# Four small moves in the first third of an attention-and-FFN kernel: one copy changes engine, three groups of loads change place

## The chip, the cores and the metric

The kernel runs on one core of a Trainium2 chip. A core has five instruction streams that run side by side and meet only through semaphores: TensorE (PE in the profile; its weight loads are listed apart as PEld), VectorE (DVE), ScalarE (ACT), GpSimd (POOL) and SyncE (SP). Each stream runs its instructions strictly in the order in which the program issues them, so an instruction that waits holds up everything behind it on its own engine and nothing on the others. Data comes in and goes out by DMA. This program issues DMAs from two places: from SP (queue q1 of the profile, "hardware_dynamic") and from POOL (queue q0, "software_dynamic"); both are served by the same 16 DMA engines. The metric is the device time of one execution in microseconds (us); lower is better.

## The reference

Two blocks follow each other. The first is attention with a selective decay, for batch 8, 8 heads, 576 positions, head dimension 64:

```python
scores = scale * np.matmul(q, k.transpose(0, 1, 3, 2))
causal = np.triu(np.ones((S, S), dtype=bool), k=1)
cum = np.cumsum(np.maximum(s, 0.0), axis=-1)
bias = -(cum[:, :, :, None] - cum[:, :, None, :])
scores = np.where(causal, -1000000000.0, scores + np.minimum(bias, 0.0))
attn = softmax(scores)
attn_out = np.matmul(attn, v)
```

Its output, 4608 rows of 512, goes into a gated FFN with inner width 1536:

```python
g = x @ w_gate
val = x @ w_val
out = (silu(g) * val) @ w_out
```

## The kernel before

**Attention.** The 64 (batch, head) pairs are numbered 0 to 63, and four of them make a group; there are 16 groups, and `h` in `side` and `side_v` is the number of the group whose scores are being made, `step` (0 to 3) the pair in it, `ci` (0 to 3) the piece of that pair's scores. "k 3" or "q 3" is the k or q of group 3, "V 1" the values of batch 1. A group's k and q are loaded as f32 (`load_one`, L141), cast to bf16 (`cast_one`, L253), transposed, and copied into a tile `KQ` in SBUF that holds rows ready for the scores. For groups 0 to 4 TensorE transposes (`pe_transpose`, L295, its matmuls at L301) and `pe_out` (L319) copies the result out of PSUM, at L330 on VectorE or at L328 on ScalarE, in two halves of 64 partitions; a bank of PSUM is given back after its second half. From group 5 on the transposes are done by DMA: `scratch` (L272, L274) writes the cast tile to DRAM, `transposes` (L281, L284) reads it back transposed, and `split` (L286, L288) copies it into `KQ`. The scores are matmuls at L373, their exponentials are on ScalarE at L383 (into a tile `pt`), and GpSimd clears the masked triangles at L388 and L393.

V is loaded in five pieces a batch (`load_v`, L156): four of 128 positions (256 KB) and one of 64 (128 KB), all in rows of 256 bytes. There is one raw buffer for V, so V of the next batch can be loaded only when the last piece of the one before is cast. `cast_v` (L167) casts the pieces: V 1 and V 2 on GpSimd (L173), V 3 and later on ScalarE (L171). The weighted sums are matmuls at L410, in five parts a pair: parts 0 to 2, part 3, part 4, the last of which need V pieces 3 and 4. The result reaches the FFN's input `XT` by TensorE for batches 0 and 1 (`x_pe`, L453, L459), and later by a write to DRAM (L444) and a DMA transpose (L451).

**FFN.** The 4608 rows are taken in nine tiles of 512. For each tile 12 column blocks follow (`gate_value`, L658): four matmuls for the gate (L643), a tanh on ScalarE (`th`, L664), a multiply on VectorE (`pp`, L666), four matmuls for the value (L643), a multiply on VectorE (`ht`, L677). Then comes the down product (L700 for the first two tiles, L749 later). The weights are loaded by `w_load` (L335, issued at L346): the gate's first half in one piece (768 KB), then the value's first half in two, then the second halves of gate and value in two pieces each ("1, 0" and "1, 1", 384 KB each), then `w_out` in two of 768 KB. Column blocks 6 to 8 use the pieces "1, 0", blocks 9 to 11 the pieces "1, 1".

**Order.** The order of the instructions is written out by hand. Eight banks of PSUM are handed round (`take`, `give`): a new product gets the bank that was given back longest ago, and TensorE waits until its reader is done. A prologue (L949 to L1036) makes the first eight pairs of attention and begins the first FFN tile. After it the FFN's tiles are driven as a list of items (L1060 to L1090); after each item the loop runs at most one delayed copy (`seconds`), the hooks of that item, and then pumps the attention generator `attn_items` (L561), so that attention for later rows is woven between the FFN's matmuls. The hooks of the first tile are the transposes of k 2's second part at item 2, the casts of k 3 and q 3 on GpSimd at items 9 and 10, and the two loads of `w_out` on GpSimd's queue at items 11 and 13.

`prep_one` (L540) makes one set of a group's TensorE transposes and its first copy, and puts the second copy on the list `seconds`:

```python
pe_out(hb, nm, g, 0, eng)
seconds.append(lambda: pe_out(hb, nm, g, 1, eng))
```

Around the change, in order: V 1 is loaded from SP at L1015, followed by k, q 4 and k, q 5; V 1 is cast on GpSimd beside the scores of pairs 11 and 12 (`V1_AT`, L477); pair 8's weighted sums, the first that need V 1, follow the scores of pair 12. Later, at `h == 6`, SP issues the loads of k 9 and q 9 at step 0, the write of group 8 at step 2, the first two pieces of V 4 at step 2, the transposes of group 8 and the last three pieces of V 4 at step 3; ScalarE casts k 9 and q 9 at `h == 7`, steps 0 and 1.

Of the kernel before, what the change touches and what calls it, by code (L numbers as in the profile page):

```python
# [19 lines left out]
def kernel(  # L20
# [11 lines left out]
    nc = tc.nc  # L32
# [81 lines left out]
    with tc.manual_schedule():  # L114
# [16 lines left out]
        def give(b):  # L131
            clock[0] += 1
            released[b] = clock[0]
# [7 lines left out]
        def load_one(hb, name, rs=(0, NR), eng=nc.sync):  # L141
            b, g = divmod(hb, 2)
            if rs[0] == 0:
                loaded[name, hb] = raw.tile([128, NR, J, D], FP32, tag="raw" + name, name="raw" + name)
            eng.dma_start(
                loaded[name, hb][:, rs[0] : rs[1], :, :].rearrange("x r j d -> x r (j d)"),
                SRC[name][0][b, g * HB + 2 * rs[0] : g * HB + 2 * rs[1], :, :].rearrange(
                    "(r e) (p j) d -> (e p) r (j d)", e=2, j=J
                ),
            )  # L150

        def load_qk(hb):
            load_one(hb, "k")
            load_one(hb, "q")

        def load_v(b, cs, eng=nc.sync):  # L156
            if 0 in cs:
                loaded["v", b] = raw.tile([128, NCH, H, D], FP32, tag="rawv", bufs=1, name="rawv")
            t = loaded["v", b]
            for c in cs:  # L160
                n = 128 if c < 4 else TAIL
                eng.dma_start(  # L162
                    t[0:n, c, :, :],
                    v[b, :, c * 128 : c * 128 + n, :].rearrange("h p d -> p h d"),
                )
# [153 lines left out]
        def pe_out(hb, name, g, r, eng):  # L319
            j0, j1 = JG[g]  # L320
            kq = SRC[name][1]
            dst = KQ[hb % 2][r][64 * r : 64 * r + 64, kq, 0 : NR * S].rearrange(
                "a (x j) -> a x j", j=J
            )[:, :, j0:j1]
            tp = tps[name, g]
            srcp = tp[0][64 * r : 64 * r + 64].rearrange("a j x -> a x j")
            if eng is nc.scalar:
                nc.scalar.copy(dst, srcp)  # L328
            else:
                eng.tensor_copy(dst, srcp)  # L330
            tp[2] -= 1
            if tp[2] == 0:
                give(tp[1])

        def w_load(kind, j, h=None):  # L335
            dst = {"g": WG, "v": WV, "o": WO}[kind][j]
            if kind == "o":
                src_ap = moe_w_out[j * WKO * 128 : (j + 1) * WKO * 128, :].rearrange(
                    "(c p) n -> p c n", p=128
                )  # L340
            else:
                w = moe_w_gate if kind == "g" else moe_w_val
                lo, hi = (0, WCH) if h is None else (h * WCH // 2, (h + 1) * WCH // 2)
                src_ap = w[:, j * WCH + lo : j * WCH + hi].rearrange("(c p) n -> p c n", p=128)
                dst = dst[:, :, lo:hi]
            nc.gpsimd.dma_start(dst, src_ap)  # L346
# [124 lines left out]
        def do_later(n):  # L471
            while n > 0 and later:
                f, *args = later.pop(0)
                f(*args)
                n -= 1
# [5 lines left out]
        def side(h, step, ci):  # L481
            bh = HB * h + step
            for c in V1_AT.get((bh, ci), ()):
                cast_v(1, c, nc.gpsimd)
            if bh == H + 4 and ci == 3:
                load_v(2, range(5))
            if h == 4 and (step, ci) in ((0, 1), (2, 1)):
                load_qk(6 + step // 2)
            if h >= 5 and h + 3 < NHB and (step, ci) == (0, 1):
                load_qk(h + 3)  # L490
            hb = h + 1
            if NPE <= hb < NHB:
                late = hb == NPE
                if late and (step, ci) == (0, 1):
                    scratch(hb)
                if late and (step, ci) == (0, 3):
                    transposes(hb)
                if (step, ci) == (0, 1):
                    aug(hb, GP4)
                first = 1 if hb < NPE + 3 else 0  # L500
                if step in (first, first + 1) and ci == (3 if late else 1):
                    for r in range(NR):
                        later.append((split, hb, "kq"[step - first], r))
            hb = h + 2
            if hb == NPE and step == 3 and ci % 2 == 1:
                cast_one(hb, "kq"[ci // 2], nc.gpsimd)
            if NPE < hb < NHB:
                six = hb == NPE + 1
                if (step, ci) == ((2, 0) if six else (0, 2)):
                    cast_one(hb, "k", nc.scalar)  # L510
                if (step, ci) == ((2, 2) if six else (1, 2)):
                    cast_one(hb, "q", nc.scalar)
                if (step, ci) == ((3, 0) if six else (2, 0)):
                    scratch(hb)
                if (step, ci) == (3, 3 if six else 0):
                    do_later(NR * 2)
                    transposes(hb)
            if ci != 1:
                return
            bn = h // 2 + 1  # L520
            if 3 <= bn < B:
                if h % 2 == 0:
                    if step == 2:
                        load_v(bn, (0, 1))
                    if step == 3:
                        load_v(bn, (2, 3, 4))

        V2_AT = {(1, 0): 0, (1, 1): 1, (1, 2): 2, (1, 3): 3, (2, 0): 4}
# [1 line left out]

        def side_v(h, step, ci):
            bn = h // 2 + 1
            if h == 4 and (step, ci) in V2_AT:
                cast_v(2, V2_AT[step, ci], nc.gpsimd)
            if 3 <= bn < B and h % 2 == 1 and (step, ci) in V_AT:
                cast_v(bn, V_AT[step, ci], nc.scalar)

        seconds = []

        def prep_one(hb, i, eng=None):  # L540
            g, nm = divmod(i, 2)
            nm = ("k", "q")[nm]
            pe_transpose(hb, nm, g)
            if eng is None:
                eng = nc.scalar if nm == "k" else nc.vector
            pe_out(hb, nm, g, 0, eng)
            seconds.append(lambda: pe_out(hb, nm, g, 1, eng))

        PREP_AT = {
            2: {(1, 3): 0, (2, 1): 2, (2, 3): 1, (3, 1): 3},  # L550
# [432 lines left out]
        load_one(2, "q", eng=nc.gpsimd)  # L983
        w_load("v", 0, 0)
        w_load("v", 0, 1)
        for nm in ("g", "v"):
            w_load(nm, 1, 0)
        load_one(3, "k", eng=nc.gpsimd)
        scores(1)
        half_batch("k")  # L990
        score_piece(2, 0)
# [9 lines left out]
        aug(2, SP4)  # L1001
        cast_one(2, "k", nc.gpsimd)
        cast_one(2, "q", nc.gpsimd)
        load_one(3, "q", eng=nc.gpsimd)
        for nm in ("g", "v"):
            w_load(nm, 1, 1)
        init_vt(1)
# [21 lines left out]
            seconds.pop(0)()  # L1029
        for ft in range(3):  # L1030
            begin("g", ft, range(2, 3))
        for i in (1, 3):
            prep_one(2, i)
        first_sbuf.close()
        PTP[0] = ctx.enter_context(tc.tile_pool(name="later", bufs=1))
        PTP["bufs"] = 5  # L1036
# [85 lines left out]
```

## Time and profile before

| what | value |
|---|---|
| times of three runs | 373.49, 375.02, 375.54 us; median 375.02 us |
| the profiled execution's own time | 374.06 us |
| its span, first to last instruction | 372.1 us |
| busy: PE, DVE, ACT, POOL | 361.0, 289.8, 240.9, 212.3 us |
| mean granted TensorE clock | 0.998 |
| DMA packets, and those under 512 B | 97134, 77229 |

The span is what the trace covers; what lies outside it is 1.96 us. Times inside the trace are counted from the start of the span. An entry of the chain of waits or of the timeline has its start, its length, the engine and the line; a bracket at its end tells how long the engine had been idle and what ended that. An entry for a DMA queue has the number of packets, the megabytes and the share of the 16 engines' time. One row of V is a packet of 256 bytes.

### The profile page before, as it was taken

Reading aid. Unit: us, or ns where it says so; the run is one execution under the profiler, and the core shown is the slowest. Engines: PE = TensorE matmul, PEld = TensorE weight load, DVE = VectorE, ACT = ScalarE, POOL = GpSimd, SP = SyncE. Lnnn points to the kernel's source line nnn. Section 1 sums busy time; section 2 is a strip of 40 time slices with the busy share of each in tenths; the row PEclk is TensorE's granted clock in tenths of the full one; section 3 lists DMA queues with packets and bytes.
Section 4 is the critical chain, followed back from the end, with each engine's and each line's share of the span. In section 5 each row is a group of like instructions: output and inputs, shape, how many; then the busy total and the mean of one; then the engine's idle time right before and its main releaser. Section 6 shows DMA issues by size and latency. Waiting matters only on the chain.

```text
span 372.1 us, 8744 instructions
## 1 busy us (share of the span) xinstructions
PE 361.0 (97%) x3248; PEld 230.3 (62%) x3288; DVE 289.8 (78%) x584; ACT 240.9 (65%) x471; POOL 212.3 (57%) x325
## 2 busy tenths in 40 slices
PE   7799999999999999999999999999999999999996
PEld 6574557655555557855685558655865585476465
DVE  8878776377995999589967897699868867975984
ACT  8877776788885977688757875786565523323321
POOL 7984555956266647594749464955675516315320
PEclk9999999999999999999999999999999999999999
DMA  7999999799979996896789575995142113002003
GB/s 241 200 256 258 217 261 267 215 315 225 273 153 322 220 247 185 152 300 211 214 179 263 166 192 166 252 177 138 40 121 62 35 29 119 0 2 87 28 0 113
DMA packets 97134, 64.21 MB, mean 173 GB/s; under 512 B 77229, under 2 KB 82725, under 8 KB 97093
## 3 DMA queue, kind: packets, MB, share of 16 engines
q1 hardware_dynamic: 84964, 41.46, 46.7%
q0 software_dynamic: 12128, 22.21, 23.2%
q8 instruction: 25, 0.41, 0.5%
q14 instruction: 17, 0.13, 0.1%
HBM read 37.90 MB, written 19.86 MB: 155 GB/s over the span
## 4 chain that ended last, share of the span: by engine, by line
PE 86%; DVE 5%; POOL 3%; ACT 2%; issue 1%; DMA 1%; SPq 0%; DVEq 0%; ACTq 0%; POOLq 0%
PE banks L643 45%; PE banks L749 17%; PE banks L373 10%; PE banks L410 8%; PE banks L700 5%; DVE kq L330 2%; DVE pp L666 1%; DMA rawk<-in_k_dram 1%; POOL rawv L162 1%; DVE ht L677 1%; POOL vt L173 1%; PE banks L301 1%; ACT pt L383 1%; PE banks L459 1%; ACT th L664 0%
## 5 line engine op out<-in xcount | busy, mean ns | idle before, releaser
L383 ACT ACTIVATE pt<-banks 128x512 bf16<-128x512 f32 (+1 forms) x256 | 120.5, 509 | 29.2 <-PE banks L373 16.8
L643 PE MATMUL banks<-XT,wg 128*128 128x512 bf16 x418 | 110.3, 379 | 1.2 <-DVE pp L666 0.3
L643 PE MATMUL banks<-XT,wv 128*128 128x512 bf16 x412 | 109.3, 379 | 1.1
L664 ACT ACTIVATE th<-banks 128x512 bf16<-128x512 f32 x108 | 64.7, 599 | 56.2 <-PE banks L643 50.3
L666 DVE SCALAR_TENSOR_TENSOR pp<-th,banks 128x512 bf16<-128x512 bf16 x108 | 73.6, 682 | 18.5 <-ACT th L664 18.0
L677 DVE SCALAR_TENSOR_TENSOR ht<-pp,banks 128x512 bf16<-128x512 bf16 x108 | 74.1, 686 | 10.3
L373 PE MATMUL banks<-kq 128*128 128x128 bf16 (+4 forms) x576 | 76.5, 240 | 0.9 <-DVE kq L330 0.3
L686 POOL TENSOR_TENSOR ht<-ht 128x512 bf16<-128x512 bf16 x35 | 40.4, 1154 | 52.3 <-DVE su L684 52.2
L373 PEld LDWEIGHTS <-kq 128*128 128x128 bf16 x576 | 46.1, 98 | 30.5 <-issue 1.7
L643 PEld LDWEIGHTS <-wv 128*128 128x128 bf16 x432 | 38.4, 98 | 36.2 <-issue 0.2
L643 PEld LDWEIGHTS <-wg 128*128 128x128 bf16 x432 | 38.3, 98 | 34.2 <-issue 0.7
L410 PEld LDWEIGHTS <-pt 128*128 128x128 bf16 x960 | 41.9, 98 | 17.1
L388 POOL TENSOR_SCALAR_AFFINE_SELECT pt<-pt 128x512 bf16<-128x512 bf16 x56 | 36.9, 658 | 25.8 <-ACT pt L383 21.9
L410 PE MATMUL banks<-vt,pt 128*128 128x65 bf16 x960 | 46.9, 194 | 0.1
L444 POOL DMA_DIRECT2D xs<-ot x24 | 21.7, 904 | 30.5 <-DVE ot L427 28.2
L749 PEld LDWEIGHTS <-ht 128*128 128x128 bf16 x336 | 31.2, 98 | 4.3
L427 DVE TENSOR_TENSOR ot<-banks,rc 128x320 bf16<-128x320 f32 x64 | 31.5, 492 | 2.2
L188 POOL DMA_DIRECT2D kq<-HL x48 | 28.9, 605 | 0.0
L749 PEld LDWEIGHTS <-su 128*128 128x128 bf16 x252 | 23.5, 98 | 3.3
L700 PE MATMUL banks<-wo,ht 128*128 128x512 bf16 x90 | 24.8, 379 | 0.3
L814 POOL TENSOR_TENSOR ysb<-ysb 128x512 f32<-128x512 f32 x12 | 15.2, 1270 | 15.3 <-DVE ysb L808 15.3
L749 PE MATMUL banks<-WS,ht 128*128 128x256 bf16 x168 | 22.9, 273 | 0.0
(101 smaller groups left out, 376.7 us busy)
## 6 DMA issues: line engine op xcount, KB each, us to landing
out_dram<-ysb POOLq DMA_DIRECT2D x32, 256.0 KB, 4.0
rawv<-in_v_dram SPq DMA_DIRECT2D x28, 256.0 KB
rawk<-in_k_dram SPq DMA_DIRECT2D x12, 576.0 KB
rawq<-in_q_dram SPq DMA_DIRECT2D x12, 576.0 KB
xs<-ot POOLq DMA_DIRECT2D x24, 160.0 KB, 4.0
ks<-ck SPq DMA_DIRECT2D x11, 288.0 KB
qs<-cq SPq DMA_DIRECT2D x11, 288.0 KB
rawk<-in_k_dram POOLq DMA_DIRECT2D x3, 576.0 KB, 5.6
```

Of the source, the lines that this page charges most:

```text
L373: nc.tensor.matmul(sc[:, o : o + w], T[:, 1, e * S + 128 * tj : e * S + 128 * (tj + 1)], T[:, 0, e * S + lo : e * S + hi], start=not maske ...
L383: nc.scalar.activation(pt[:, c0 : c0 + n], sc, AF.Exp, scale=0.125)
L388: nc.gpsimd.affine_select(pt[:, 1088:1600], pt[:, 1088:1600], pattern=[[0, 4], [1, 128]], compare_op=ALU.is_ge, fill=zreg, base=0, channel ...
L410: nc.tensor.matmul(av[:, bi * (D + 1) : (bi + 1) * (D + 1)], pt[:, c0 : c0 + 128], VT[b % 2][:, tj, h, :], start=(tj == 0), stop=(tj == bi),)
L427: nc.vector.tensor_mul(ot[:, :, e * D : (e + 1) * D], av3[:, :, 0:D], rc[:, :, None].to_broadcast([128, NCH, D]),)
L643: nc.tensor.matmul(view(bs, TT), w[:, c, f0 : f0 + 128], xt[:, c, :], start=(c == 0), stop=(c == 3),)
L664: nc.scalar.activation(th, pg, AF.Tanh, scale=0.5)
L666: nc.vector.scalar_tensor_tensor(pp, in0=th, scalar=1.0, in1=pg, op0=ALU.add, op1=ALU.mult)
L677: nc.vector.scalar_tensor_tensor(hp[:, 2 * k2 : 2 * k2 + 2, :].rearrange("p a n -> p (a n)"), in0=pp, scalar=0.5, in1=pv, op0=ALU.mult, op ...
L686: (nc.vector if ft == NFT - 1 else nc.gpsimd).tensor_sub(hp[:, 1:3, :], hp[:, 1:4:2, :], hp[:, 0:3:2, :])
L700: nc.tensor.matmul(view(pys[ts_], DM), hps[ft // 2][:, 2 * (ft % 2) + half, c0 : c0 + 128], WO[j][:, ft % WKO, :], start=(ft == 0), stop=( ...
L749: nc.tensor.matmul(ps, lhs(p), rhs(p), start=(first and p == 0), stop=(last and p == NP - 1), skip_group_check=True,)
```

## The change

Four things are edited. (1) `prep_one` takes a second engine for the second copy; the last of q 2's copies, of the second 64 partitions of its second part, is made by ScalarE where VectorE made it. (2) The loads of k 3 and q 3 on GpSimd's queue are both issued after the value weights' first half and in front of the third pieces of the gate and the value ("1, 0"); before, k 3 stood behind these two pieces, and q 3 behind the casts of k 2 and q 2. (3) The first two pieces of V 4 are loaded at the last score piece of `h == 5`, in place of `h == 6`, step 2. (4) q 9 is loaded at `h == 6`, step 3, in front of the last three pieces of V 4; before, it was loaded at step 0, right behind k 9, which stays there.

```diff
@@ side
             if h >= 5 and h + 3 < NHB and (step, ci) == (0, 1):
-                load_qk(h + 3)
+                if h == 6:
+                    load_one(h + 3, "k")
+                else:
+                    load_qk(h + 3)
...
             if 3 <= bn < B:
                 if h % 2 == 0:
-                    if step == 2:
+                    if step == 2 and h != 6:
                         load_v(bn, (0, 1))
                     if step == 3:
+                        if h == 6:
+                            load_one(h + 3, "q")
                         load_v(bn, (2, 3, 4))
@@ side_v
             bn = h // 2 + 1
+            if h == 5 and (step, ci) == (3, 3):
+                load_v(4, (0, 1))
@@ prep_one
-        def prep_one(hb, i, eng=None):
+        def prep_one(hb, i, eng=None, eng2=None):
...
-            seconds.append(lambda: pe_out(hb, nm, g, 1, eng))
+            seconds.append(lambda: pe_out(hb, nm, g, 1, eng2 or eng))
@@ the prologue
         w_load("v", 0, 0)
         w_load("v", 0, 1)
+        for nm in ("k", "q"):
+            load_one(3, nm, eng=nc.gpsimd)
         for nm in ("g", "v"):
             w_load(nm, 1, 0)
-        load_one(3, "k", eng=nc.gpsimd)
         scores(1)
...
         cast_one(2, "k", nc.gpsimd)
         cast_one(2, "q", nc.gpsimd)
-        load_one(3, "q", eng=nc.gpsimd)
...
-        for i in (1, 3):
-            prep_one(2, i)
+        prep_one(2, 1)
+        prep_one(2, 3, None, nc.scalar)
```

## The prediction

> **What bounds the kernel now.** I read the page's busy times and chain first, then TensorE's waits, then each place where the change acts.
>
> ```profile
> PE 361.0 (97%) x3248; PEld 230.3 (62%) x3288; DVE 289.8 (78%) x584; ACT 240.9 (65%) x471; POOL 212.3 (57%) x325
> PE 86%; DVE 5%; POOL 3%; ACT 2%; issue 1%; DMA 1%; SPq 0%; DVEq 0%; ACTq 0%; POOLq 0%
> ```
>
> TensorE bounds the whole, so an edit is worth what it takes from, or adds to, TensorE's waits. Between 26 and 300 us the view of waits shows only three for it, 0.3 us each. The timeline places the two that matter:
>
> ```profile
> 33.43 0.38 PE L373 MATMUL banks<-kq 128*128 128x320 bf16 x2 [0.31 <-DVE kq L330]
> 34.15 1.02 PE L643 MATMUL banks<-XT,wg 128*128 128x512 bf16 x3 [0.34 <-DVE pp L666]
> ```
>
> The chain of waits (start, length, what) shows why: from 29 to 35.5 us it runs through VectorE, whose copies and products give back the banks that TensorE waits for. Its later lines show a second weak place at 52 us.
>
> ```profile
> 29.03 1.44 DVE kq L330 x2
> ...
> 32.66 0.72 DVE kq L330
> ...
> 33.41 0.70 DVE pp L666
> ...
> 34.20 0.69 DVE ht L677
> ...
> 34.89 0.61 DVE pp L666
> ...
> 35.54 1.89 PE banks L643 x8
> ...
> 50.89 1.13 POOL vt L173 x2
> ...
> 52.06 0.19 PE banks L410
> ```
>
> The copy at 32.66 is the one that edit 1 moves. The last two lines say that pair 8's weighted sums wait for GpSimd's cast of V 1: V 1 has almost nothing to spare.
>
> GpSimd's timeline shows what edit 2 removes, two casts that wait for their loads, and what stands behind them on that engine: the first load of w_out.
>
> ```profile
> 37.96 1.14 POOL L260 CAST ck<-rawk 128x1152 bf16<-128x1152 f32 x1 [0.79 <-DMA rawk<-in_k_dram]
> ...
> 39.41 1.15 POOL L260 CAST cq<-rawq 128x1152 bf16<-128x1152 f32 x1 [0.30 <-DMA rawq<-in_q_dram]
> ...
> 40.69 0.85 POOL L346 DMA_DIRECT2D wo<-in_moe_w_out_dram  x1
> ```
>
> Last, the DMA view in three stretches. From 34 to 42 us the two queues get the same number of packets, whatever their size:
>
> ```profile
> q0 software_dynamic: 1243, 1.83, 91.7%
> q1 hardware_dynamic: 1252, 0.31, 27.1%
> ```
>
> From 42 to 44.5 us POOL's queue has run nearly dry (the weights are in, w_out's rows not yet there), and V 1, on q1, rushes through:
>
> ```profile
> q1 hardware_dynamic: 1669, 0.42, 79.7%
> q0 software_dynamic: 233, 0.18, 46.2%
> ```
>
> From 46 to 50 us w_out and V 1's last piece alternate again:
>
> ```profile
> q0 software_dynamic: 635, 0.63, 93.6%
> q1 hardware_dynamic: 547, 0.18, 28.5%
> ```
>
> **Edit 1, the copy.** It takes one 64x512 copy off VectorE (0.72 us, the row at 32.66) and puts one on ScalarE (0.72 us, L328's rows of 64x512). Everything VectorE does behind it moves up by that and its 0.03 us of issue: the product at 33.41 to 32.66. On ScalarE the copy falls between the tanh that ends at 30.24 and the k 2 copy at 30.56, so the two tanhs behind (31.15, 32.50) end at about 32.15 and 33.50. The first is early enough for the product at 32.66; the second allows the next product at about 34.15 in place of 34.81. TensorE's block at 35.54, which waited for that product, starts at about 34.87: a gain of 0.67, call it 0.65. ScalarE is back in step at the tanh of 37.52, before which it idles 1.05 us. Bounds: 0 if ScalarE's 0.4 us lateness reaches the banks, 1.0 if both waits and the gap at 35.5 vanish.
>
> **Edit 2, the order of loads.** Two 576 KB loads pass two of 384 KB. GpSimd issues the same instructions; k 2's cast moves 0.75 us back (one issue), to end near 25.4, while the cast of q 2 waits for its load until 26.41 anyway: cost nothing. "1, 0" of the gate and value, issued at 21.31 and 22.04, landed 12.1 and 14.1 us later (33.4, 36.2); behind k 3 and q 3 that is some 3.2 us later (those two landed 1.7 and 1.5 us apart, 37.9 and 39.4 by issue plus 15.1 and 11.9), so 36.6 and 39.4. TensorE needs them at 40.82 and 42.34, or 0.65 sooner: 2.3 us of cover at the tightest; if it were gone, TensorE would stand by the shortfall. k 3 and q 3 are in before 35 us, the casts follow GpSimd's mask work at about 36.5 and 37.6, the mask at L393 must await ScalarE to about 38.85, and the first w_out load is issued at about 39.1 in place of 40.69. The casts' waits themselves cost TensorE nothing; without the edit they would eat about half of edit 1's gain.
>
> But the earlier w_out load speaks against the change. Before, its first rows move about 2.8 us after its issue, near 43.5; now from about 42, when the queue still holds weights. The hole closes, and V 1 keeps taking turns. By 42 us V 1 has had about 2,250 of its 4,608 packets (2,282 of q1 from 28 to 42, a few of them other). In front of it stand some 150 weight packets and w_out's 1,536, at 635 in 4 us: 10.6 us, to 52.6. V 1 gets as many turns less a little, some 1,500 to 1,690, and the rest (670 to 850) at the 667 per us of the hole: the last piece is in at about 53.8, where before it was in at 50 (547 more packets of q1 by then). Its cast, the third of the casts from 50.84, started at about 52.0 and would with edit 1 start at 51.3; now it starts at 53.8 and ends 0.6 later. TensorE's part 4 of pair 8 began at 52.95 and now begins at about 54.45: 1.5 us later than before, with edit 1's gain already in it. Piece 3 says the same: its last packet passes near 52.8, its cast ends at 53.5, and part 3, which began at 52.06, begins 1.5 late. Behind it, k 4 and q 4 come after V 1 on q1: GpSimd already waits for them at 54.44 (1.61 us) and 56.95 (1.36 us), and they too slip, by no more than 1.5 to 2 us. What comes later is bound by TensorE and moves along. Bounds: -0.65 (half of the hole survives; 0.75 us of lateness is enough to close it, and I expect 1.6), and +2.6 if V 1's last engine ends 1 us after the others, as k 4's cast suggests: it starts 1.7 us after k 4's last packets near 52.7.
>
> The Trainium skill ("DMA: Bandwidth & Descriptors", "Latency and other measured facts") puts the first byte of such a software-issued DMA about 1 us after its issue. By that w_out would have been in the queue at 41.7 before, no hole would have been there to lose, and the sum would be edit 1's alone, 373.9; the packets from 42 to 44.5 us show the hole, so the trace speaks against it here.
>
> **Edits 3 and 4.** Near 113 to 127 us TensorE waits for nothing, so no gain. V 4's two issues (1.83 us at 113.18) go in front of XT's transposes at 105.90, and q 9's 0.46 us leaves 109.06; SP is then about 1.3 us late at L451, covered by the 1.6 us between the last such packets (115.5) and the FFN tile that reads them (117.10). q 9 now follows SP's transposes of group 8 (issues from 118.32 to 123.16), so it is issued near 121.5 to 123, behind their packets, and lands near 125 to 127; its cast runs at 126.77 on ScalarE. Cost: 0 to 1 us of ScalarE, which idles 0.6 to 0.8 us at a time there; I take 0, as the nearest rows (k 9 and q 9 both through in 5 us from 108.43) land it just in time. V 4's last three pieces stand behind q 9 but are cast only from 131.37.
>
> **The sum.** The profiled execution took 374.06 (span 372.1 and 1.96 around it). Edit 1: -0.65; V 1 late: +2.15; the rest 0: +1.5, 375.6. The median shown is 0.96 above that execution; the mean of all four executions is 374.5, and with +1.5 I forecast 376.0.
>
> **The rivals.** *The hole doesn't matter* (not slower): w_out starts no earlier than V 1 can bear, and edit 1's gain stays: 374.5 - 0.65 = 373.9. For it: half of the hole is enough; against it: the wait of GpSimd is plainly in front of the load. It decides at a w_out issue about 0.5 us earlier than before; from 0.75 the hole is gone. The skill's rule above belongs here. *ScalarE starves at q 9*: SP's transposes go at 118.32 as before, q 9 lands at 127.5 or later, ScalarE holds scores and tanhs for 1 to 2 us, and TensorE loses up to that: on top of V 1's, 377.5. For it: a load with some 5 us for a way that took 5; against it: ScalarE idles there. *Edit 1 does nothing*, because ScalarE's own tanhs come 0.4 late: 375.2 without V 1's loss, inside the first rival's range.
>
> **How the numbers follow.** V 1 late 0.50, hole harmless 0.38, q 9 late 0.12. A measurement of this kernel tells about 0.5% (1.9 us) from no change, so faster is under 373.1 and slower over 376.9. V 1 late spans 374.4 to 377.8 (its bounds): a third of it, 0.16, is slower, 0.34 within. The harmless case spans 372.8 to 375: 0.16 faster, 0.22 within. q 9 late: 0.09 slower, 0.03 within. Together 0.16, 0.59, 0.25. The range for 8 in 10 is 373.2 to 377.8; the likeliest case alone has 374.4 to 377.8.
>
> **What would show it.** Edit 1: a 64x512 copy on ScalarE near 30.3, TensorE's block of 35.54 at 34.9. Edit 2: no waits at the two casts; w_out issued near 39; q1 no more than about 500 packets from 42 to 44.5; GpSimd's cast of V 1 waiting for its load, and TensorE's parts of pair 8 near 54. If V 1's casts still run without a wait near 51, my main term is wrong and the first rival holds. Edits 3 and 4: a wait of ScalarE for q 9's load shows the second; none shows them free.

## The result and the profile after

The changed kernel takes 378.95 us (median of 18 executions, 375.74 to 382.69); the kernel before, beside it on the same chips, 374.99 us (18 executions, 373.49 to 377.93). The ratio is 1.0098, with a 95% interval of 1.007 to 1.0126: 1% slower, where the forecast was 376.0 and the range ended at 377.8. The ratio leaves out the longest of the 18, which is more than 1.5% above the fastest. The profiled execution took 379.14 us, with a span of 377.2.

The page after. TensorE is as busy as before to within 0.7 us, but the chain now has 7% on DMA, nearly all of it waiting for V (the third line lists the chain by line, cut by the page itself to the costliest):

```profile
PE 361.7 (96%) x3248; PEld 230.8 (61%) x3288; DVE 289.6 (77%) x583; ACT 241.3 (64%) x472; POOL 212.7 (56%) x325
PE 83%; DMA 7%; DVE 4%; SPq 2%; ACT 2%; issue 1%; DVEq 0%; POOL 0%
PE banks L650 43%; PE banks L756 17%; PE banks L373 10%; PE banks L410 7%; DMA rawv<-in_v_dram 6%; PE banks L707 5%; SPq L162 2%; DVE kq L330 2%; DMA rawq<-in_q_dram 1%; DVE ht L684 1%; DVE pp L673 1%; DVE kq L288 0%; ACT kq L328 0%; PE banks L367 0%; ACT pt L383 0%
```

(Lines behind the edits have shifted: L643 is now L650, L664 L671, L666 L673, L677 L684; L162, L173, L373, L383, L410 kept their numbers.) TensorE's waits, with total, number and longest, have one new entry, larger than all the others:

```profile
PE banks L410 <- POOL vt L173: 4.7, 1, 4.7
```

The chain after names what it hangs on (start, length, what). A single piece of V 1 is in flight for 22.5 us, from SP's issue at 32.36 to 54.84, then come its cast and pair 8's part 3:

```profile
25.96 6.36 SPq L162
...
32.36 22.48 DMA rawv<-in_v_dram
54.84 0.05 issue
54.90 0.63 POOL vt L173
...
55.56 0.21 PE banks L410
```

GpSimd's timeline after (start, length, instruction; in brackets the idle time before it and what ended it) shows cause and effect on one engine. The two casts at 36.71 and 37.80 no longer wait, w_out's first load is out at 39.08 instead of 40.69, and the fourth and fifth casts of V 1 wait 4.60 and 0.66 us. Before, the last three casts ran in one go without a wait; this is their line before, and then the lines after:

```profile
50.84 1.72 POOL L173 CAST vt<-rawv 128x512 bf16<-128x512 f32 x3
```

```profile
36.71 1.14 POOL L260 CAST ck<-rawk 128x1152 bf16<-128x1152 f32 x1
37.80 1.15 POOL L260 CAST cq<-rawq 128x1152 bf16<-128x1152 f32 x1
...
39.08 0.84 POOL L346 DMA_DIRECT2D wo<-in_moe_w_out_dram  x1
...
54.90 0.62 POOL L173 CAST vt<-rawv 128x512 bf16<-128x512 f32 x1 [4.60 <-DMA rawv<-in_v_dram]
56.17 0.61 POOL L173 CAST vt<-rawv 64x512 bf16<-64x512 f32 x1 [0.66 <-DMA rawv<-in_v_dram]
```

TensorE's timeline at the same place, before and then after. After, there are 4.71 us of idleness, then four matmuls of the FFN that take 1.89 us, as against 1.03 a few us earlier, and part 4 of pair 8 at 57.28:

```profile
52.09 1.02 PE L643 MATMUL banks<-XT,wv 128*128 128x512 bf16 x4
...
52.95 0.78 PE L410 MATMUL banks<-vt,pt 128*128 128x65 bf16 x20
```

```profile
48.23 1.03 PE L650 MATMUL banks<-XT,wv 128*128 128x512 bf16 x4
...
55.56 0.21 PE L410 MATMUL banks<-vt,pt 128*128 128x65 bf16 x1 [4.71 <-POOL vt L173]
55.59 1.89 PE L650 MATMUL banks<-XT,wv 128*128 128x512 bf16 x4
57.28 1.31 PE L410 MATMUL banks<-vt,pt 128*128 128x65 bf16 x20
```

Why they take longer stands in the view by windows (from:to, length, busy time and count of PE, PEld, DVE, ACT, POOL, then the granted TensorE clock, DMA share, GB/s). The wait itself passes at full clock, and the work after it gets half of it:

```profile
52.00:55.50 3.50, 0.00 (x0) 0.00 (x0) 0.00 (x0) 0.00 (x0) 0.60 (x1) 0.98 1.14 278
55.50:57.00 1.50, 1.44 (x5) 0.61 (x5) 0.00 (x0) 0.00 (x0) 0.81 (x3) 0.50 1.05 381
57.00:58.50 1.50, 1.50 (x24) 1.23 (x23) 0.94 (x3) 0.00 (x0) 0.99 (x1) 0.50 1.06 392
58.50:60.00 1.50, 1.50 (x13) 0.90 (x11) 0.93 (x3) 0.69 (x2) 1.21 (x2) 0.92 1.12 335
```

To compare executions I measure from one event to another, since the time at which pair 7 is reached differs by some 3 us between these traces (24.0 to 27.2 us): from the first exponential of the last score piece of pair 7 to the first of pair 20. That stretch contains what edits 1 and 2 act on and the whole of V 1's way.

| kernel | from pair 7 to pair 20 | against before | w_out issued ahead of the last weights' landing | TensorE's waits for V 1's casts |
|---|---|---|---|---|
| before | 59.92 us | | 4.07 us | none |
| after | 65.19 | +5.27 | 5.99 | 4.7 |
| edit 1 alone | 59.04 | -0.88 | 1.1 | none |
| order of edit 2 alone | 64.21 | +4.29 | 5.03 | 1.9 and 0.9 |
| edits 3 and 4 alone | 59.92 | 0.00 | 4.07 | none |
| after, w_out behind the mask | 59.47 | -0.45 | 3.3 | none |
| before, w_out in front of the casts | 63.26 | +3.34 | 6.75 | 3.0 |
| after, w_out later | 59.04 | -0.88 | 3.67 | none |

The fourth column is the time from the issue of w_out's first load to the landing of the last weight piece, "1, 1" of the value, as the trace has them (before: 40.69 and 44.76; after: 39.08 and 45.07).

From pair 7 to the end of the span the changed kernel loses 5.33 us (347.52 before, 352.85 after), so what lies beyond pair 20 adds next to nothing to it: the loss arises between 50 and 59 us.

### The profile page after: what moved, and what is told of

Same layout as the page of the kernel before. It is cut to its first block, busy times and chain, and to the rows that moved or that the text cites. A ratio compares the mean times of both kernels' runs of the same rounds, so it can differ in the third digit from the quotient of the medians.

```text
span 377.2 us, 8743 instructions
## 1 busy us (share of the span) xinstructions
PE 361.7 (96%) x3248; PEld 230.8 (61%) x3288; DVE 289.6 (77%) x583; ACT 241.3 (64%) x472; POOL 212.7 (56%) x325
## 2 busy tenths in 40 slices
DMA packets 97133, 64.21 MB, mean 170 GB/s; under 512 B 77228, under 2 KB 82724, under 8 KB 97092
## 3 DMA queue, kind: packets, MB, share of 16 engines
q1 hardware_dynamic: 84964, 41.46, 45.5%
## 4 chain that ended last, share of the span: by engine, by line
PE 83%; DMA 7%; DVE 4%; SPq 2%; ACT 2%; issue 1%; DVEq 0%; POOL 0%
PE banks L650 43%; PE banks L756 17%; PE banks L373 10%; PE banks L410 7%; DMA rawv<-in_v_dram 6%; PE banks L707 5%; SPq L162 2%; DVE kq L330 2%; DMA rawq<-in_q_dram 1%; DVE ht L684 1%; DVE pp L673 1%; DVE kq L288 0%; ACT kq L328 0%; PE banks L367 0%; ACT pt L383 0%
## 5 line engine op out<-in xcount | busy, mean ns | idle before, releaser
L383 ACT ACTIVATE pt<-banks 128x512 bf16<-128x512 f32 (+1 forms) x256 | 120.5, 511 | 34.3 <-PE banks L373 15.7
L650 PE MATMUL banks<-XT,wv 128*128 128x512 bf16 x412 | 110.2, 381 | 1.1
L650 PE MATMUL banks<-XT,wg 128*128 128x512 bf16 x418 | 110.3, 379 | 0.8
L671 ACT ACTIVATE th<-banks 128x512 bf16<-128x512 f32 x108 | 64.7, 599 | 54.8 <-PE banks L650 49.5
L673 DVE SCALAR_TENSOR_TENSOR pp<-th,banks 128x512 bf16<-128x512 bf16 x108 | 73.7, 682 | 19.4 <-ACT th L671 18.9
L684 DVE SCALAR_TENSOR_TENSOR ht<-pp,banks 128x512 bf16<-128x512 bf16 x108 | 74.2, 687 | 16.1 <-PE banks L650 5.6
L373 PE MATMUL banks<-kq 128*128 128x128 bf16 (+4 forms) x576 | 76.3, 240 | 0.4 <-DVE kq L288 0.3
L373 PEld LDWEIGHTS <-kq 128*128 128x128 bf16 x576 | 46.2, 98 | 30.0 <-issue 1.6
L650 PEld LDWEIGHTS <-wv 128*128 128x128 bf16 x432 | 38.5, 98 | 41.2 <-issue 5.6
L650 PEld LDWEIGHTS <-wg 128*128 128x128 bf16 x432 | 38.4, 98 | 33.8 <-issue 0.2
L410 PEld LDWEIGHTS <-pt 128*128 128x128 bf16 x960 | 42.4, 98 | 17.5 <-issue 0.5
L410 PE MATMUL banks<-vt,pt 128*128 128x65 bf16 x960 | 47.3, 195 | 4.8 <-POOL vt L173 4.7
L427 DVE TENSOR_TENSOR ot<-banks,rc 128x320 bf16<-128x320 f32 x64 | 31.5, 492 | 2.2
L393 POOL TENSOR_SCALAR_AFFINE_SELECT pt<-pt 128x64 bf16<-128x64 bf16 x56 | 14.9, 265 | 16.3 <-ACT pt L383 16.2
```

The lines of the kernel that those rows point to most:

```text
L373: nc.tensor.matmul(sc[:, o : o + w], T[:, 1, e * S + 128 * tj : e * S + 128 * (tj + 1)], T[:, 0, e * S + lo : e * S + hi], start=not maske ...
L383: nc.scalar.activation(pt[:, c0 : c0 + n], sc, AF.Exp, scale=0.125)
L410: nc.tensor.matmul(av[:, bi * (D + 1) : (bi + 1) * (D + 1)], pt[:, c0 : c0 + 128], VT[b % 2][:, tj, h, :], start=(tj == 0), stop=(tj == bi),)
L427: nc.vector.tensor_mul(ot[:, :, e * D : (e + 1) * D], av3[:, :, 0:D], rc[:, :, None].to_broadcast([128, NCH, D]),)
L650: nc.tensor.matmul(view(bs, TT), w[:, c, f0 : f0 + 128], xt[:, c, :], start=(c == 0), stop=(c == 3),)
L671: nc.scalar.activation(th, pg, AF.Tanh, scale=0.5)
```

## The experiments

The theory is that of the prediction: w_out's first load, issued earlier, meets the last weights in POOL's queue, the pause in that queue disappears, and V 1 goes on sharing the DMA engines with it (*the pause*; the prediction calls it the hole, the expectations theory 1). The rivals are that the new order of the loads of k 3, q 3 and the weights itself delays V 1 or the casts (*the order*, theory 2), that q 9 comes late, and that the copy costs more on ScalarE than it frees on VectorE. The expectations name some kernels by a label: e4_wout_after_mask is "after, w_out behind the mask" in the table above, e6_wout_first "before, w_out in front of the casts", e7_wout_late "after, w_out later", and e11_all_late and e12_all_late_warm are the pair of the section on the clock.

### Each edit alone

Edit 1, on the kernel before:

```diff
-        for i in (1, 3):
-            prep_one(2, i)
+        prep_one(2, 1)
+        prep_one(2, 3, None, nc.scalar)
```

> The kernel before with the copy on ScalarE alone. Theory 1 (the hole: the loss comes from w_out's first load, which follows the weights without a gap, so that V 1 keeps taking turns) and theory 2 (the order: the loss comes from k 3 and q 3 standing in front of the third weight pieces while V 1 starts) both expect no loss here: w_out's first load is issued near 40.7 us as before, since the casts of k 3 and q 3 still wait for their loads; V 1's casts run near 51 us without a wait; TensorE's block of 35.54 us starts at about 34.9; in the end 0.2 to 0.7 us faster than before (ratio 0.998 to 1.000).

Measured: 374.69 us (10 executions), ratio 1.0006 (0.9977 to 1.0035); in the trace the stretch is 0.88 us shorter. The copy earns something, but 0.24% of the time cannot be read from an interval of 0.6%.

Edit 2, on the kernel before:

```diff
         w_load("v", 0, 1)
+        for nm in ("k", "q"):
+            load_one(3, nm, eng=nc.gpsimd)
         for nm in ("g", "v"):
             w_load(nm, 1, 0)
-        load_one(3, "k", eng=nc.gpsimd)
...
-        load_one(3, "q", eng=nc.gpsimd)
```

> The kernel before with the earlier place of k 3 and q 3 alone. Both theories expect most of the loss: theory 1 because w_out's first load goes out near 39.7 us (1.0 us sooner, since the casts no longer wait), so that the last piece of V 1 lands near 55 us and TensorE stands about 2 to 4 us in pair 8's weighted sums: 2.5 to 4 us slower than before (ratio 1.007 to 1.011). If the loss needs the copy's edit too, this kernel stays within 0.5 us of before.

Measured: 379.14 us (4 executions), ratio 1.0123 (1.0068 to 1.0178), and +4.29 us in the stretch. V 1's last two casts on GpSimd's timeline of this kernel wait:

```profile
52.74 0.62 POOL L173 CAST vt<-rawv 128x512 bf16<-128x512 f32 x1 [1.81 <-DMA rawv<-in_v_dram]
54.81 0.61 POOL L173 CAST vt<-rawv 64x512 bf16<-64x512 f32 x1 [1.45 <-DMA rawv<-in_v_dram]
```

So the loss belongs to edit 2 alone. It does not yet say by which of the two theories.

Edits 3 and 4, on the kernel before:

```diff
-                load_qk(h + 3)
+                if h == 6:
+                    load_one(h + 3, "k")
+                else:
+                    load_qk(h + 3)
...
-                    if step == 2:
+                    if step == 2 and h != 6:
                         load_v(bn, (0, 1))
                     if step == 3:
+                        if h == 6:
+                            load_one(h + 3, "q")
...
+            if h == 5 and (step, ci) == (3, 3):
+                load_v(4, (0, 1))
```

> The kernel before with V 4's first two pieces sooner and q 9 later, alone. Theories 1 and 2 expect nothing (within 0.5 us of before, ratio 0.998 to 1.002): nothing near 105 to 135 us waits for a DMA. The rival that q 9 comes late expects a wait of ScalarE for q 9's load near 127 us and 1 to 2 us more.

Measured: 374.01 us (10 executions), ratio 1.0003 (0.997 to 1.0036), and from pair 7 to the end 347.50 us as against 347.52. They cost and gain nothing. In the changed kernel's ScalarE timeline the cast of q 9 runs without a wait, as its line has no bracket:

```profile
131.76 1.14 ACT L258 CAST cq<-rawq 128x1152 bf16<-128x1152 f32 x1
```

### The order of the loads, or the time of w_out

Two kernels part the theories. The first keeps all of the changed kernel, and with it the order, and only issues w_out later, behind the mask that follows the casts:

```diff
-        at_item(11, w_load, "o", 0)
-        at_item(13, w_load, "o", 1)
+        at_item(13, w_load, "o", 0)
+        at_item(14, w_load, "o", 1)
```

> The changed kernel, its two loads of w_out moved from items 11 and 13 to items 13 and 14, behind one mask of GpSimd: issued near 40.5 and 41.4 us in place of 39.1 and 40.5. Nothing else differs, so k 3 and q 3 stand in front as in the changed kernel. Theory 1 expects the hole back (some 1,400 to 1,700 packets of q1 from 42 to 44.5 us), V 1's casts near 50 us with little or no wait, and 373.5 to 374.5, that is 0.5 to 1.2 us faster than before. Theory 2 expects V 1 as late as in the changed kernel, 3 to 4 us slower than before.

The second keeps the order of the kernel before and issues both loads of w_out in front of the casts of k 3 and q 3:

```diff
+        at_item(8, w_load, "o", 0)
+        at_item(8, w_load, "o", 1)
...
-        at_item(11, w_load, "o", 0)
-        at_item(13, w_load, "o", 1)
```

> The kernel before, only its two loads of w_out moved in front of the casts of k 3 and q 3 (from items 11 and 13 to item 8): issued near 37 and 38 us in place of 40.7 and 42.1; k 3 and q 3, the copy and V 4 stay as they were. Theory 1 expects that this alone makes the loss, since w_out then follows the weights without a gap: V 1's third and fourth casts wait for their loads to 53 to 56 us, and 3.5 to 5.5 us more than before (ratio 1.010 to 1.015). Theory 2 (the order of k 3 and q 3) expects no change (ratio 0.998 to 1.002).

With the order kept and w_out later: 374.22 us (10 executions), ratio 0.9985 (0.9962 to 1.0008). GpSimd's timeline shows V 1's last three casts in one run without a wait; what the later w_out costs is probably seen at k 4 and q 4, whose casts wait 2.38 and 1.83 us (1.61 and 1.36 before) while half of the copy's 0.88 us is given back:

```profile
50.68 1.72 POOL L173 CAST vt<-rawv 128x512 bf16<-128x512 f32 x3
...
55.05 1.14 POOL L260 CAST ck<-rawk 128x1152 bf16<-128x1152 f32 x1 [2.38 <-DMA rawk<-in_k_dram]
58.01 1.15 POOL L260 CAST cq<-rawq 128x1152 bf16<-128x1152 f32 x1 [1.83 <-DMA rawq<-in_q_dram]
```

With the old order and w_out early: 378.34 us (5 executions), ratio 1.0073 (1.0042 to 1.0104), +3.34 us in the stretch (3.5 to 5.5 and a ratio of 1.010 to 1.015 had been expected). The same wait as in the changed kernel is there:

```profile
36.69 1.67 POOL L346 DMA_DIRECT2D wo<-in_moe_w_out_dram  x2
...
54.30 1.29 POOL L173 CAST vt<-rawv 128x512 bf16<-128x512 f32 x2 [2.98 <-DMA rawv<-in_v_dram]
```

The DMA view from 42 to 44.5 us (queue: packets, MB, share) of the first, where the pause is whole, and of the second, where it is gone and the queues alternate packet for packet:

```profile
q1 hardware_dynamic: 1463, 0.37, 74.1%
q0 software_dynamic: 282, 0.21, 52.7%
```

```profile
q0 software_dynamic: 403, 0.38, 91.2%
q1 hardware_dynamic: 406, 0.10, 31.2%
```

The order without the early w_out loses nothing, and the early w_out without the order loses: the early w_out, which takes the pause away, is the cause, the order is not.

### How late, and on which engines

The changed kernel's own count in this window lies between those two:

```profile
q0 software_dynamic: 331, 0.27, 66.1%
q1 hardware_dynamic: 1140, 0.29, 60.0%
```

Yet its V 1 was the latest of them. The marks that each of the 16 DMA engines leaves when it is through with its part of a transfer explain this:

| kernel | V 1, 4th piece: engines done in time, and the last | 5th piece: the last |
|---|---|---|
| before | 16 between 43.9 and 46.0 | 50.5 |
| after | 7 by 45.5; the other 9 late, last at 54.84 | 56.1 |
| order of edit 2 alone | 13 by 44.7; 47.6, 49.6, 52.7 | 54.76 |
| before, w_out in front of the casts | none; all between 51.97 and 54.25 | 54.93 |
| after, w_out behind the mask | 16 by 46.14 | 51.0 |
| after, w_out later | 16 by 45.64 | 50.29 |

The pause is not one pause but 16, one on each DMA engine, and a piece of V has landed only when the slowest engine is done. The marks do not carry an engine's name, but their number shows which engines lose the pause: count the engines whose last mark for the weights comes more than 4.2 us after the issue of w_out's first load. There are 9 in the changed kernel, 3 with edit 2 alone, 3 in the kernel with 64 matmuls of the next section, all 16 in the three kernels with w_out in front of the casts (two of them follow in the next section), and none in the other seven traces. In each of the 13 this is the number of engines on which V 1's fourth piece is late; the nearest marks on either side are at 4.17 us (in time) and 4.28 us (late). A sum over the engines does not show it: with edit 2 alone q1 carried 1474 packets from 42 to 44.5 us, with w_out later 1469, and one lost 4.29 us by V 1 and the other nothing. "DMA: Bandwidth & Descriptors" in the Trainium skill states both halves: each engine takes turns between its queues on its own (section "Queues, rings and completion order"), and the 16 engines finish independently, only the full count meaning that the data is there ("Why a DMA increments its semaphore by 16 and not by 1"); the marks above agree, with 9.3 us between the last of the earlier seven engines and the last of all for one 256 KB piece.

What goes with it is the fourth column of the table above: in every kernel with w_out up to 4.07 us ahead of the last weights' landing V 1 is in time, and in every one from 4.67 us on (the first kernel of the next section) it is late.

### What the halved clock costs

To take the halved clock away, 64 small matmuls whose result nobody reads keep TensorE busy ahead of part 3 of pair 8; first on the changed kernel:

```diff
+                        if p == H:
+                            wb = take()
+                            keep_warm(64, wb)
+                            give(wb)
```

> The changed kernel with 64 matmuls of 128 columns on the identity (extra work, about 3.5 us, whose result nobody reads) on TensorE in front of part 3 of pair 8's weighted sums, inside the wait for V 1's cast. If half of the changed kernel's late loss is TensorE's clock (granted 0.50 for 3.4 us after the wait), the clock stays at 1.0, the time from 51 to 60 us is about 1.5 us shorter, and the whole 1 to 1.7 us faster than the changed kernel where V 1 is as late (some 376.5 to 378 us, ratio to before 1.004 to 1.009). If the clock plays no part, the same time as the changed kernel or, where V 1 comes sooner, up to 3 us more.

Measured: 377.66 us (10 executions), ratio 1.0076 (1.0048 to 1.0104), 62.41 us in the stretch. The clock stayed at 1.0 in the trace, but V 1's last piece also came sooner in this execution (52.92 us, three engines late, w_out 4.67 us ahead of the last weights), so the difference from the changed kernel is no price of the clock. The pair was repeated with w_out in front of the casts, where every engine is late and the lateness differs little between executions, without and with the 64 matmuls:

```diff
+        at_item(8, w_load, "o", 0)
+        at_item(8, w_load, "o", 1)
...
-        at_item(11, w_load, "o", 0)
-        at_item(13, w_load, "o", 1)
```

> The changed kernel with both loads of w_out at item 8, in front of the casts of k 3 and q 3, so that V 1 is late on all 16 DMA engines and TensorE idles some 4 us in front of part 3 of pair 8. Paired with e12_all_late_warm to price the clock. If the clock falls after such a wait, it is granted 0.50 for 3.4 us and the time from pair 7's last exponential to pair 20's first is 64 to 65.5 us; if it doesn't fall, about 63.3 us as in e6_wout_first. Ratio to before 1.008 to 1.015.

> e11_all_late with 64 matmuls of 128 columns on the identity (extra work that nobody reads) in front of part 3 of pair 8, inside TensorE's wait. If the clock is part of the loss, it stays at 1.0 here and the time from pair 7's last exponential to pair 20's first is 0.8 to 1.5 us shorter than e11_all_late's, V 1 landing at the same time; if it is not, the two agree within 0.2 us.

Without them: 380.56 us (4 executions), ratio 1.0135 (1.0076 to 1.0194), 66.51 us in the stretch, a wait of 3.5 us and then half a clock for 6.83 us. With them: 378.2 us (10 executions), ratio 1.0073 (1.0037 to 1.0109), 64.96 us in the stretch. The windows of the one and of the other (the clock is the third number from the end):

```profile
54.00:56.00 2.00, 0.39 (x2) 0.16 (x2) 0.00 (x0) 0.00 (x0) 1.03 (x2) 0.68 1.05 354
56.00:58.00 2.00, 2.00 (x17) 1.13 (x16) 0.43 (x1) 0.00 (x0) 1.42 (x3) 0.50 1.06 393
58.00:60.00 2.00, 2.00 (x19) 1.30 (x17) 1.44 (x5) 0.60 (x1) 1.45 (x3) 0.50 1.09 360
```

```profile
54.00:56.00 2.00, 2.00 (x30) 1.60 (x28) 0.00 (x0) 0.00 (x0) 0.62 (x1) 1.00 1.06 349
56.00:58.00 2.00, 0.82 (x22) 0.65 (x20) 0.88 (x3) 0.00 (x0) 0.80 (x2) 1.00 1.06 391
58.00:60.00 2.00, 2.00 (x21) 1.08 (x18) 1.08 (x3) 1.22 (x3) 1.46 (x2) 1.00 1.11 343
```

The extra work makes the kernel 1.55 us faster in the trace, although V 1's last piece landed 1.3 us later in that execution (56.83 as against 55.53). The intervals of the two ratios overlap, but all four executions without the matmuls (380.15 to 381.0 us) are slower than all ten with them (377.2 to 379.07). So the halved clock is a price of its own, on top of the wait.

### Keeping the copy without the loss

The changed kernel with w_out's first load back at about its old time and the second one behind V 1's casts:

```diff
-        at_item(11, w_load, "o", 0)
-        at_item(13, w_load, "o", 1)
+        at_item(13, w_load, "o", 0)
+        at_item(22, w_load, "o", 1)
```

> The changed kernel with its loads of w_out at items 13 and 22: the first behind one mask as in e4_wout_after_mask, the second behind V 1's casts, near 52 us. Theory 1 expects V 1's casts without a wait, and k 4 and q 4 sooner than in e4_wout_after_mask, since the second load no longer takes turns with them: GpSimd's casts of k 4 and q 4 wait under 1 us together, and the copy's gain of 0.88 us, which e4_wout_after_mask gave half back near 55 us, is kept to the end: 0.6 to 0.9 us faster than before (ratio 0.9975 to 0.9985). If w_out's second half comes too late, TensorE waits near 64 us and it is slower than that by the wait.

Measured: 373.18 us (12 executions, 372.69 to 375.08), ratio 0.996 (0.994 to 0.9979): 0.4% faster than the kernel before, with an interval that lies below 1. On GpSimd's timeline V 1, the second w_out and k 4 follow each other without a wait:

```profile
50.08 1.72 POOL L173 CAST vt<-rawv 128x512 bf16<-128x512 f32 x3
...
52.05 0.84 POOL L346 DMA_DIRECT2D wo<-in_moe_w_out_dram  x1
52.88 1.16 POOL L260 CAST ck<-rawk 128x1152 bf16<-128x1152 f32 x1
```

Whether edit 2 has any part in this gain was asked by two more kernels: the kernel before with edit 1 and the later second load, and the kernel before with that later load alone (its first load stays at item 11).

```diff
-        at_item(13, w_load, "o", 1)
+        at_item(22, w_load, "o", 1)
```

> The kernel before with the copy on ScalarE and the second load of w_out at item 22 in place of 13; k, q 3 and V 4, q 9 as before. It asks what the earlier k 3 and q 3 add to e7_wout_late (ratio 0.996). If they add nothing, this kernel is as fast: 0.995 to 0.998, and the time from pair 7's last exponential to pair 20's first is 59.0 us, 0.88 under before. If the casts of k 3 and q 3, which wait for their loads here, hold TensorE's transposes near 39 us, about 0.4 us of the copy's gain are lost: 59.4 us and a ratio of 0.997 to 0.999.

> The kernel before with the second load of w_out at item 22 in place of 13, and nothing else. It asks whether e7_wout_late's 1.5 us came from this move. In the kernel before TensorE waits for nothing near 50 to 60 us, so that I expect 0 to 0.5 us (ratio 0.9985 to 1.000), and 59.9 us from pair 7's last exponential to pair 20's first. If the move is the main part, a ratio of 0.996 to 0.998 as for e7_wout_late.

Measured: 374.17 us (12 executions), ratio 0.998 (0.9944 to 1.0016), and 374.66 us (12 executions), ratio 0.9971 (0.9938 to 1.0005). In the traces the stretch is 59.03 us with edit 1 and 59.92 without: 0.89 shorter and unchanged. With the old order the casts of k 3 and q 3 still wait 0.44 and 0.30 us, and TensorE does not feel it. So edit 2 adds nothing that the traces show; the intervals of the times are too wide to part the three kernels.

## Why the prediction was wrong

**Right: the path.** The forecast's likeliest case was V 1 late, and each of its signs but two came in, the count of q1's packets and the time of pair 8's parts (pair 7 is 0.28 us early in this execution, so 0.28 is added to compare with the clock of before): the two casts without a wait at 36.99 and 38.08 (36.5 and 37.6 forecast), w_out issued at 39.36 (39.1), GpSimd's cast of V 1 waiting for its load. The pieces "1, 0" of the weights landed at 36.9 and 39.56 by the span (36.6 and 39.4), early enough. In the clock of before part 3 of pair 8 began at 55.84 and part 4 at 57.56, where 53.6 and 54.45 were forecast. That the hole is gone with 0.75 us of lateness fits: V 1 was in time with w_out 4.07 us ahead of the last weights, and late with 4.67. The rivals by which the hole does not matter, or ScalarE starves at q 9, are refuted, and so is the one by which edit 1 does nothing.

**Edit 1 was better than its term** (-0.88 us as against -0.65, within its bounds of 0 and -1.0). ScalarE's timeline after has the copy as the first of the two that begin at 30.22, 30.50 in the clock of before (30.24 forecast); it had to await VectorE's copy of the first half:

```profile
30.22 1.45 ACT L328 COPY kq<-banks 64x512 bf16<-64x512 bf16 x2 [0.27 <-DVE kq L330]
31.55 0.58 ACT L671 ACTIVATE th<-banks 128x512 bf16<-128x512 f32 x1
32.16 0.72 ACT L328 COPY kq<-banks 64x512 bf16<-64x512 bf16 x1
32.90 0.60 ACT L671 ACTIVATE th<-banks 128x512 bf16<-128x512 f32 x1
```

The two tanhs end at 32.13 and 33.50, in the clock of before 32.41 and 33.78, and thus 0.3 us later than forecast (32.15 and 33.50). It did no harm: TensorE's block of 35.54 starts at 34.38, or 34.66 in the clock of before, where 34.87 was forecast.

**The step that failed is the term "V 1 late: +2.15".** In the profiled execution it measures +6.15 (5.27, and the copy's 0.88 that it swallowed). Two things were missing.

1. *The landing.* The prediction counted the packets of all 16 engines in one sum and divided by the sum of their turns, which gives the time of an average engine: last piece in and cast from 53.8. The cast began at 56.17, 56.45 in the clock of before, 2.65 us later. The mean of the 16 marks of that piece is 53.56, 53.84 in the clock of before, so the average engine came as forecast; but that was luck, since the forecast took the pause from all engines and seven kept it. Where all 16 had lost it (w_out in front of the casts, old order) the mean was 54.10 and the last engine 54.93, 54.53 and 55.36 in the clock of before. The prediction had written "if V 1's last engine ends 1 us after the others" as a bound; the spread between engines was not 1 us but 9.3 on the fourth piece. Even the sign named for it, q1 under 500 packets from 42 to 44.5 us, was wrong for that reason: 1140 passed, most of them, it seems, on the engines that still had their pause. It had also read the weights as in at 42 us, when the marks of their last piece run from 42.24 to 44.76 before, and expected w_out's rows to move from about 42. By the size of the rows (768 bytes for the weights, 1024 for w_out) the first of w_out's moved at 43.52 after, as against 43.54 before, although the load was issued 1.6 us sooner; what differs is that nine engines ended their weights only at 43.74 or later, when w_out's rows were already moving on others.
2. *The clock.* The prediction priced the wait as idle time alone. Behind it TensorE ran at 0.50 for 3.41 us (from 55.33). V 1's last cast ended at 56.78, but part 4, behind the slowed FFN block, began at 57.28 instead of about 56.83: 0.45 us. Its 20 matmuls then took 1.31 us instead of 0.78, and by the end of the slow stretch 0.66 us had been lost. Together 1.1 us.

2.65 and 1.1 make 3.75; with the +1.5 of the forecast that is 5.25, and 5.27 was measured. "TensorE: Matmul & The Clock Gate" in the Trainium skill ("Part 1: The HAM clock gate") says that an idle window of about 3.4 us drops the clock to half, and that about 3.4 us of work bring it back. The trace agrees, 0.50 for 3.41 us behind 4.71 us of idleness; what the forecast lacked is a term for it: 1.1 us here.

The range had a slip of its own: its bounds of -0.65 and +2.6, put on the mean of 374.5 from which the sum starts, give 373.9 and 377.1, not 374.4 and 377.8. The measured 378.95 is outside of both.

**From one execution to the median.** The median lost 3.96 us, the profiled execution 5.1. The executions' mean granted clock sorts them: 0.5 for 3.41 us is 0.45% of the span, for 6.83 us 0.9%. Of the 17 executions of the changed kernel that are in the ratio two show 1.000 (375.74 and 377.65 us), ten 0.994 or 0.995 (mean 378.9) and five 0.989 to 0.991 (mean 379.9). The two whose clock was not lowered are within the range that was forecast; the other fifteen average 2.5 us more. That need not be the price of the clock alone, since an execution with a longer wait may also lose its clock more often, which was not measured apart; the pair with and without the 64 matmuls gives 1.55 us in the trace and 2.4 between the medians.

**Left open.** Why the line between an engine that keeps its pause and one that loses it lies near 4.2 us, and what moves the end of the weights between executions, was not found. The 0.4% of the best kernel is more than the 0.24% that the copy shows, and in its own trace only 0.13 us are left from pair 7 to the end (347.39 as against 347.52). 12 of 76 executions of the kernel before that ran beside the experiments had a clock under 0.996, and none of the best kernel's 12; that the kernel before at times loses its clock, or V 1's margin, would fit, but it has not been seen in a trace. The later second load of w_out does not by itself prevent it: the kernel before with that load alone has none under 0.998 in 12 executions, but with edit 1 added 4 of 12 are under 0.996 (the kernel with w_out behind the mask: 3 of 10). Edit 1 alone, edit 2 alone and the best kernel lose another 0.6 to 0.8 us between pairs 48 and 56 in their traces, which the others do not; only these three have a wait of TensorE between 200 and 300 us, 0.3 to 0.4 us for VectorE's products at L427, whose cause is not shown.

## What to carry to other kernels

A cast that no longer waits also releases what stands behind it on its engine, and if that is a DMA issue, it must be asked which transfer it will now meet and who has been living on the pause. Estimate a landing by the slowest DMA engine and not by the sum over all: two kernels whose total counts agreed landed a piece 7 us apart (52.7 and 45.6). And a wait that leaves TensorE busy for about a third or less of one of the clock's 3.41-us windows (next section) is paid twice, once as idleness and once at half clock, so a late load can cost more than its lateness.

## What was not expected of the hardware

- Idleness of 4.7 us brought 0.50 of the clock for 3.41 us, idleness of 3.5 us 0.50 for 6.83 us, and idleness of 3.0 us (w_out in front of the casts, old order) nothing; two waits of 1.9 and 0.9 us with 1.2 us of work between them were enough in the kernel with edit 2 alone, where the clock was at 0.50 for 3.41 us from 54.98. So a wait's length alone does not decide it.
- What decides it can be read from the traces. In all 13 of them every stretch between two changes of the clock is a whole multiple of 3.413 us (15, 1 and 93 of these windows in the changed kernel). The clock fell at the end of each of the 12 windows of this grid in which TensorE was busy for 35% of the time or less, three of them around V 1's wait: 0% from 51.92 to 55.33 in the changed kernel, 34% with edit 2 alone, 24% with the wait of 3.5 us. It fell after none of the 1380 others within the spans, which have 46% or more; the wait of 3.0 us was spread over two windows of 46 and 66%. Between 35 and 46% lies no window, and what makes the half clock last one window or two is not shown. The Trainium skill's page on the clock, named above, calls the window in which activity is counted free-running; the traces agree: the window that holds most of the wait begins 27.6 us after pair 7 in the changed kernel, 27.5 with edit 2 alone, 26.9 for the 3.5 us and 26.2 for the 3.0 us. Where a wait falls on the grid is thus one reason why executions of one kernel differ.
- 64 additional matmuls in front of a wait made the kernel 1.55 us faster in the trace.
- Of the 16 engines of one 256 KB load seven ended by 45.53 us and nine from 49.49 to 54.84 us.
